# 224 unused bytes ahead of the activation tiles of a fused attention and feed-forward kernel

## The chip, the cores and the metric

The kernel runs on one core of one Trainium2 chip. The metric is the time of one execution on the device in microseconds. Lower is better. Engines are called PE (TensorE's matmuls), PEld (TensorE's weight loads), DVE (VectorE), ACT (ScalarE), POOL (GpSimd) and SP (SyncE, which issues the transfers).

## What is computed

Causal attention of 8 batches, 8 heads, 576 positions and 64 features, four heads with a local mask and four with a strided one, and behind it a feed-forward layer on 4608 tokens of 512 features with a hidden width of 2048:

```python
    scores = np.where(masks[None, :, :, :], scores, -1000000000.0)
    scores = scores - np.max(scores, axis=-1, keepdims=True)
    attn = np.exp(scores)
    attn = attn / (np.sum(attn, axis=-1, keepdims=True) + 1e-09)
    return np.matmul(attn, v).astype(np.float32)
...
    h = x @ w_in
    g = h * (1.0 / (1.0 + np.exp(-1.702 * h)))
    return (g @ w_out).astype(np.float32)
```

## The kernel before

The feed-forward layer is the bulk. Its tokens are cut into 9 groups of 512 (`NG`, `G`), its hidden width into 16 slices of 128 (`NF`), which makes 144 steps (`steps`, one for each group and slice). Every operand of a product is split into a high and a low part of type float32r, and a product is the sum of three matmuls (high with high, and each low part with the other's high part).

In step s, `ffn1` (line 474) makes the hidden slice `h`: 12 matmuls into one bank of the accumulator, 4 chunks of the features times 3 products. The stationary operand is a 128 by 128 piece of a weight tile `w`, the moving operand 512 tokens of `x` (tiles `xhl`, `xll`, `xhs`, `xls`: high or low part, local or strided heads). `act` (line 490) makes the activation in the tile `g2`, ACT first and DVE behind it; `split` (line 498) makes its high part `gh` on ACT and its low part `gl` on DVE. Two steps later (`LAG`), `ffn2` (line 506) multiplies it by the second weights: 12 matmuls, 4 pieces of 128 tokens times 3 products, into four banks `o`. Here the stationary operand is a piece of `gh` or `gl`, and the moving operand 512 columns of a weight tile `w`:

```python
            for m, (w, x) in enumerate(((wih, xh), (wih, xl), (wil, xh))):
                matmul(
                    hps[s], lhsT=w[f][:, c, :], rhs=x,
...
            for m, (g, w) in enumerate(((gh, woh), (gh, wol), (gl, woh))):
                matmul(
                    outs[i], lhsT=g[:, at], rhs=w[f],
```

So all 3456 large matmuls, 1728 named `h` and 1728 named `o` in the profile, have the same shape and type: 128 by 128 stationary, 128 by 512 moving. Each of them has a weight load of its own, which runs beside the matmul ahead of it.

The order of the work is written out by hand: every instruction is kept in program order on its engine (`InOrder`, line 106). A step of the main loop (line 652) issues `ffn1(s)`, then the work of ACT and DVE, then `ffn2(s - 2)`. The attention (`scores`, `maxima`, `softmax`, `transpose`, `values`) is cut into 42 pieces that are spread over the steps of the group before the one that needs them. The weights come as raw words, which ACT and DVE turn into the `w` tiles in the first 16 steps.

Tiles come from pools that lie one behind the other in each partition: const, wp, st, io, small, ffn. Within a pool the tiles lie in the order in which the code first asks for them. The build of this kernel places them as follows (first bytes in a partition, and what is left of them after division by 512):

| tiles | pool | bytes each | first bytes | modulo 512 |
|---|---|---|---|---|
| xhl, xll, xhs, xls | const | 8192, 8192, 12288, 12288 | 20192, 28384, 36576, 48864 | 224 |
| w, 32 buffers (also raw words, and the first q, k, v) | wp | 4096 | 61664 to 188640 | 224 |
| qk, 2 buffers | st | 4608 | 192736, 197344 | 224 |
| v, 2 buffers | io | 4096 | 210144, 214240 | 224 |
| nmax, ssum, rinv, 3 buffers each | small | 32 | 218336 to 218592 | 224 to 480 |
| g2 | ffn | 2048 | 218624 | 0 |
| gh, 2 buffers | ffn | 2048 | 220672, 222720 | 0 |
| gl, 2 buffers | ffn | 2048 | 224768, 226816 | 0 |

The nine small tiles take 288 bytes, which moves the byte from 224 to 0. All pieces that are read as an operand of a large matmul (512 bytes of `w`, `gh` or `gl` as the stationary one, 2048 bytes of `x` or `w` as the moving one) begin at a multiple of 512 bytes from the start of their tile.

Of the kernel before, what the change touches and what calls it, by code (L numbers as in the profile page):

```python
# [9 lines left out]
F32 = mybir.dt.float32  # L10
# [8 lines left out]
P = 128  # L19
# [44 lines left out]
def _pairs():  # L64

    def strided(b):
        return [("s", b, c) for c in range(len(NR))]

    def local(j):
        return [("l", LG * j + i, 0) for i in range(LG)]

    windows = []
    for j in range(NG - 1):
        a, b = strided(j + 1) if j + 1 < B else [], local(j + 1)
        windows.append([u for i in range(len(NR)) for u in a[i : i + 1] + b[i : i + 1]])
    return strided(0) + local(0) + [u for w in windows for u in w], windows
# [3 lines left out]
def attn_ffn(ctx, tc, lqk, sqk, lv, sv, w_in, w_out, masks, out):  # L82
# [7 lines left out]
    ffn = ctx.enter_context(tc.tile_pool(name="ffn", bufs=2))  # L90
# [8 lines left out]

    def st4(shape, dtype, name):  # L100
        return st.tile(shape, dtype, tag="st4", name=name, bufs=2)

    pairs, windows = _pairs()
    n0 = N0
# [27 lines left out]
    def load_qk(p):  # L132
        if p < len(pairs) and p not in qks:
            kind, a, c = pairs[p]
            src, n = (lqk[a], QKW[0]) if kind == "l" else (sqk[a * len(NR) + c], QKW[1])
            if p < N0 and kind == "s":
                qks[p] = w_tile([P, n], F32, f"qk_{p}")
            else:
                qks[p] = st4([P, QKW[0]], F32, f"qk_{p}")
            for i in (slice(0, n // 2), slice(n // 2, n)) if p == 0 else (slice(0, n),):  # L140
                sync.dma_start(out=qks[p][:, i], in_=src[:, i])
# [652 lines left out]
```

## Time and profile before

| | us |
|---|---|
| median of 3 runs | 907.83 (907.79 to 908.03) |
| span of the profiled execution | 905.2 |
| PE busy in it | 894.6 (99%) |
| DVE busy | 462.5 (51%) |
| ACT busy | 374.5 (41%) |

The span runs from the first to the last instruction of the program in one profiled execution; the median is 2.6 us above it, for what lies around it. Matmuls are pipelined and their shown ends reach beyond the start of the next one, so the time that a matmul takes in a dense row of them is read from one start to the next and not from its duration. The page gives every instruction the line of the helper that keeps the order (L116), so groups are told apart by the names of their tiles.

### The profile page before, as it was taken

What the parts mean: (1) busy time and instruction counts of PE and PEld (TensorE: products, weight loads), DVE (VectorE), ACT (ScalarE), POOL (GpSimd) and SP (SyncE); (2) the same over time, 40 slices, a digit from 0 to 9 for tenths busy, and PEclk for the clock granted to TensorE, in tenths of its full rate; (3) what the DMA queues carried; (4) which work ended last, traced back from release to release, by engine and by line L of the source; (5) the groups of instructions that cost most, each with busy time, mean ns of one, the idle gap of its engine ahead of it and who ended that gap; (6) DMA issues with size and microseconds to landing.
All of it is one profiled execution on the core that took longest, in us unless ns stands there. A gap on an engine that the chain in (4) does not pass through costs nothing.

```text
span 905.2 us, 14650 instructions
## 1 busy us (share of the span) xinstructions
PE 894.6 (99%) x5834; PEld 716.6 (79%) x5834; DVE 462.5 (51%) x886; ACT 374.5 (41%) x1129; POOL 55.4 (6%) x60
## 2 busy tenths in 40 slices
PE   8999999999999999999999999999999999999998
PEld 5777678888888888888888888888888888888886
DVE  4789966555454545554555555554555343323222
ACT  7798864343434333433434343434343332222221
POOL 4001001000000000010101001000001000000000
PEclk9999999999999999999999999999999999999999
DMA  9956223112121121211211211112120010001001
GB/s 277 347 214 231 76 74 104 39 39 76 51 68 38 35 76 46 57 54 44 79 39 38 78 60 58 38 42 82 33 78 23 18 47 1 1 1 47 0 1 47
DMA packets 21812, 62.42 MB, mean 69 GB/s; under 512 B 2608, under 2 KB 2992, under 8 KB 21744
## 3 DMA queue, kind: packets, MB, share of 16 engines
q1 hardware_dynamic: 21744, 61.49, 20.3%
q8 instruction: 46, 0.75, 0.3%
q14 instruction: 22, 0.18, 0.1%
HBM read 52.04 MB, written 9.44 MB: 68 GB/s over the span
## 4 chain that ended last, share of the span: by engine, by line
PE 90%; DVE 5%; ACT 3%; DMA 1%; issue 1%; DVEq 0%; ACTq 0%
PE o L116 42%; PE h L116 40%; PE a L116 4%; PE s L116 3%; DVE raw L116 1%; PE t L116 1%; ACT raw L116 1%; ACT pr L116 1%; DVE w L116 1%; DVE gl L116 1%; DMA raw<-w_out 1%; DVE pt_l L116 1%; DVE pr L116 0%; DVE pt_s L116 0%; ACT w L116 0%
## 5 line engine op out<-in xcount | busy, mean ns | idle before, releaser
L116 PE MATMUL o<-w,gh 128*128 128x512 f32 x1152 | 364.7, 398 | 0.0
L116 PEld LDWEIGHTS o<-w,gh 128*128 128x128 f32 x1152 | 213.8, 188 | 51.3
L116 DVE SCALAR_TENSOR_TENSOR g<-g,h 128x512 f32<-128x512 f32 x144 | 98.9, 687 | 268.5 <-ACT g L116 268.5
L116 PE MATMUL o<-w,gl 128*128 128x512 f32 x576 | 228.0, 396 | 0.0
L116 ACT ACTIVATE g<-h 128x512 f32<-128x512 f32 x144 | 85.9, 597 | 292.7 <-PE h L116 289.0
L116 PE MATMUL h<-xhl,w 128*128 128x512 f32 x576 | 202.9, 393 | 1.7 <-DVE w L116 0.9
L116 PE MATMUL h<-xhs,w 128*128 128x512 f32 x576 | 201.9, 391 | 0.4 <-ACT xhs L116 0.4
L116 DVE TENSOR_TENSOR gl<-g,gh 128x512 fp32r<-128x512 f32 x144 | 99.6, 692 | 129.1 <-ACT gh L116 126.7
L116 ACT CAST gh<-g 128x512 fp32r<-128x512 f32 x144 | 89.1, 619 | 184.7 <-PE o L116 176.5
L116 PEld LDWEIGHTS h<-xhl,w 128*128 128x128 f32 x576 | 107.8, 188 | 28.0 <-DVE w L116 2.4
L116 PEld LDWEIGHTS o<-w,gl 128*128 128x128 f32 x576 | 108.1, 188 | 25.9
L116 PEld LDWEIGHTS h<-xhs,w 128*128 128x128 f32 x576 | 108.2, 188 | 23.5 <-ACT xhs L116 0.8
L116 PE MATMUL h<-xll,w 128*128 128x512 f32 x288 | 112.4, 390 | 0.0
L116 PE MATMUL h<-xls,w 128*128 128x512 f32 x288 | 112.2, 389 | 0.1
L116 ACT ACTIVATE pr<-pr,nmax 128x96 f32<-128x96 f32 (+1 forms) x296 | 101.1, 346 | 0.0
L116 POOL TENSOR_TENSOR pr<-pr,rinv 128x432 f32<-128x432 f32 (+1 forms) x42 | 49.6, 1181 | 699.3 <-DVE rinv L116 699.3
L116 PEld LDWEIGHTS h<-xll,w 128*128 128x128 f32 x288 | 54.1, 188 | 11.8
L116 PEld LDWEIGHTS h<-xls,w 128*128 128x128 f32 x288 | 54.0, 188 | 11.7 <-DVE xls L116 0.4
L116 DVE STREAM_TRANSPOSE pt_l<-pr 32x256 f32<-32x256 f32 x128 | 55.5, 434 | 1.8
L116 ACT ACTIVATION_READ_ACCUMULATOR pr<-pr,nmax 128x1 f32 x296 | 56.3, 190 | 0.0
L116 DVE STREAM_TRANSPOSE pt_s<-pr 32x256 f32<-32x256 f32 x126 | 54.8, 435 | 1.8
L116 ACT ACTIVATE raw<-raw 128x512 f32<-128x512 f32 (+1 forms) x62 | 36.8, 666 | 2.4 <-DMA raw<-w_out 2.4
(64 smaller groups left out, 419.0 us busy)
## 6 DMA issues: line engine op xcount, KB each, us to landing
qk<-sqk SPq DMA_DIRECT2D x23, 452.0 KB, 4.0
qk<-lqk SPq DMA_DIRECT2D x18, 576.0 KB, 4.8
out<-out SPq DMA_DIRECT2D x36, 256.0 KB, 2.3
raw<-w_in SPq DMA_DIRECT2D x16, 512.0 KB, 8.4
raw<-w_out SPq DMA_DIRECT2D x16, 512.0 KB, 6.6
v<-lv SPq DMA_DIRECT2D x18, 384.0 KB, 3.7
v<-sv SPq DMA_DIRECT2D x24, 256.0 KB, 2.7
qk<-sqk SPq DMA_DIRECT2D x2, 226.0 KB, 2.7
```

The source lines that it names most:

```text
L116: ins = call(*args, **kw)
```

## The change

A tile of 56 float32 values (224 bytes in each partition) is asked for as the first one of the pool `ffn`. Nothing writes or reads it. The tiles `g2`, `gh` and `gl` are asked for behind it in the same pool, with tags of their own. No instruction is added, removed or moved.

```diff
     def st4(shape, dtype, name):
         return st.tile(shape, dtype, tag="st4", name=name, bufs=2)
+
+    ffn.tile([P, 224 // 4], F32, tag="fill", name="fill", bufs=1)
 
     pairs, windows = _pairs()
```

With the fill in front, `g2` would begin at byte 218848, `gh` at 220896 and 222944, `gl` at 224992 and 227040; all of these are 224 modulo 512.

## Rows read from the trace of the kernel before

**Rows 1.** The page: busy time of the engines, and the granted clock by slices.

```profile
PE 894.6 (99%) x5834; PEld 716.6 (79%) x5834; DVE 462.5 (51%) x886; ACT 374.5 (41%) x1129; POOL 55.4 (6%) x60
...
PEclk9999999999999999999999999999999999999999
```

**Rows 2.** Busy time by stretches: us, then each engine's (instructions), granted clock, DMA share, GB/s.

```profile
100.00:145.00 45.00, 43.23 (x276) 32.92 (x276) 35.00 (x64) 29.63 (x82) 3.26 (x3) 1.00 0.25 82
145.00:200.00 55.00, 55.00 (x377) 44.43 (x376) 28.84 (x61) 22.02 (x80) 3.85 (x3) 1.00 0.17 54
...
800.00:890.00 90.00, 90.00 (x392) 73.35 (x391) 23.70 (x35) 20.57 (x35) 0.00 (x0) 1.00 0.03 12
```

**Rows 3.** Matmuls of h and o by tile: ns shortest/median/longest, first and last start.

```profile
L116 PE MATMUL h<-xhs,w x120: 388/389/397, 723.1 to 887.0; 128*128 128x512 f32 x120
...
L116 PE MATMUL o<-w,gl x576: 389/396/397, 38.7 to 900.9; 128*128 128x512 f32 x192
```

**Rows 4.** Groups by line and form, PEld: busy us, mean ns of one | idle before.

```profile
L116 PEld LDWEIGHTS o<-w,gh 128*128 128x128 f32 x1152 | 213.8, 188 | 51.3
```

**Rows 5.** Timeline of PE in one step without attention: start us, us shown, what, count.

```profile
721.69 0.39 PE L116 MATMUL h<-xhl,w 128*128 128x512 f32 x1
...
722.15 0.62 PE L116 MATMUL h<-xhl,w 128*128 128x512 f32 x2
...
724.19 0.40 PE L116 MATMUL h<-xhs,w 128*128 128x512 f32 x1
724.42 0.62 PE L116 MATMUL o<-w,gh 128*128 128x512 f32 x2
724.88 0.40 PE L116 MATMUL o<-w,gl 128*128 128x512 f32 x1
...
726.98 0.40 PE L116 MATMUL o<-w,gl 128*128 128x512 f32 x1
727.22 0.39 PE L116 MATMUL h<-xhl,w 128*128 128x512 f32 x1
```

**Rows 6.** Timeline of the tail: two PE rows, and DVE's next work [idle before it].

```profile
897.41 0.40 PE L116 MATMUL o<-w,gl 128*128 128x512 f32 x1
...
898.81 0.40 PE L116 MATMUL o<-w,gl 128*128 128x512 f32 x1
...
899.25 0.69 DVE L116 TENSOR_SCALAR out<-o 128x512 f32<-128x512 f32 x1 [2.39 <-PE o L116]
```

**Rows 7.** Timeline of PE around one piece of attention.

```profile
218.57 0.73 PE L116 MATMUL o<-w,gh 128*128 128x512 f32 x2
219.14 0.40 PE L116 MATMUL o<-w,gl 128*128 128x512 f32 x1
...
221.48 0.39 PE L116 MATMUL h<-xhl,w 128*128 128x512 f32 x1
...
223.09 0.39 PE L116 MATMUL h<-xls,w 128*128 128x512 f32 x1
```

**Rows 8.** Scores from the two qk buffers: two pieces of attention, timeline of PE.

```profile
284.28 0.69 PE L116 MATMUL s<-qk 64*64 64x54 f32 x32
...
302.77 0.69 PE L116 MATMUL s<-qk 64*64 64x54 f32 x32
```

**Rows 9.** Groups by form, DVE and ACT: busy us, mean ns | idle before, what ended it.

```profile
L116 DVE TENSOR_TENSOR gl<-g,gh 128x512 fp32r<-128x512 f32 x144 | 99.6, 692 | 129.1 <-ACT gh L116 126.7
...
L116 DVE TENSOR_TENSOR xll<-a,xhl 128x512 fp32r<-128x512 f32 x16 | 11.1, 691 | 6.1 <-ACT xhl L116 6.1
...
L116 ACT CAST gh<-g 128x512 fp32r<-128x512 f32 x144 | 89.1, 619 | 184.7 <-PE o L116 176.5 <-DVE pt_s L116 7.5 <-DVE g L116 0.8
...
L116 ACT CAST w<-words 128x512 fp32r<-128x512 f32 x1 | 0.6, 620 | 1.4 <-DVE words L116 1.4
```

**Rows 10.** Waits of the whole span: who waited <- for whom: us, times, longest.

```profile
ACT g L116 <- PE h L116: 289.0, 126, 2.4
...
PE h L116 <- DVE w L116: 0.9, 3, 0.3
```

## The prediction

> **What bounds the kernel now.** I read the page first: PE is busy for 894.6 of the 905.2 us, and the granted clock is at its upper level, 2.4 GHz, in all slices [rows 1]. The table by stretches then says where PE has gaps: it is 43.23 of 45 us busy up to 145 us, and without a gap from there to 890 us [rows 2]. Of the waits, PE's own for other engines are around a microsecond each, while ACT waits 289 us for `h` [rows 10]. So from 145 us on the end is set by nothing but the time from one matmul to the next, and the 24 large matmuls of a step are nearly all of that.
>
> The question is then whether they all take the same. They have one shape and one type. The weight loads of `gh` take 188 ns [rows 4], and the five other groups of large weight loads have the same mean. In a step without attention, the third `h` matmul starts at 722.15 and the twelfth at 724.19: nine intervals in 2.04 us, 226.7 ns each. The third `o` matmul starts at 724.88 and the twelfth at 726.98: nine in 2.10 us, 233.3 ns each [rows 5]. The view by tile says the same for all of them: a matmul of `xhs` has a median of 389 ns, one of `gl` of 396 ns [rows 3]. So an `o` matmul costs 6.6 to 7 ns more than an `h` matmul, 1728 times.
>
> **Why that may hang on the byte.** What differs between `h` and `o`? I went through the candidates.
>
> - *The bank of the accumulator.* `h` stays in one bank for 12 matmuls, `o` changes it after every third. A cost of the change would fall on one interval of three. But the two intervals inside a bank, 724.42 to 724.88, already take 0.46 us, 230 ns each, against 226.7 [rows 5].
> - *Other engines on the same tiles.* DVE and ACT write `g2`, `gh` and `gl` while PE loads from them. At the end of the kernel they don't: DVE sits idle for 2.39 us up to 899.25, its work on `gl` long done, yet six `o` intervals from 897.41 to 898.81 take 1.40 us, 233.3 ns each [rows 6].
> - *Where in the partition the tile lies.* `gh` and `gl` are at the top, behind byte 220,000. The two `qk` buffers take turns, at 192,736 and 197,344, and the same 32 score matmuls take 0.69 us from either [rows 8]. That speaks against a slow region, weakly, since none of these is the region in question.
> - *The byte within 512.* For `h`, the stationary and the moving operand both begin at 224. For `o`, the moving one at 224 and the stationary one at 0. Nothing in the rows speaks against this one.
>
> One more thing speaks for operands that meet in the memory. After a change of partners the interval doesn't jump to its final value but settles: in one step with attention, the `h` matmuls start at 221.48 and only the eighth at 223.09, 230 ns each, before the pace is 226.7 again [rows 7]. A fixed cost of an instruction would not settle; two reads in step with each other would.
>
> **The change part by part.** *The fill itself* adds no instruction, no wait and no transfer; it takes 224 bytes at the end of the partition. Cost nothing, and there is no cover to lose.
>
> *DVE and ACT on the moved tiles.* DVE's `gl`, all operands at 0, takes 692 ns; its `xll`, written at 224, takes 691. ACT's `gh`, from 0 to 0, takes 619 ns; its one copy from `words` to `w`, from 224 to 224, takes 620 [rows 9]. So between a gain and a loss of 1 ns, 144 times, on engines that wait for PE: nothing.
>
> *The 1728 `o` matmuls.* Lower bound of the gain: none. Upper bound: all intervals of a step fall to 226.7 ns. A step is now 721.69 to 727.22, 5.53 us, of which 2.80 us begin with an `o` start [rows 5]. 24 times 226.7 ns is 5.44 us, 0.09 us less: 0.08 in `o`, 0.01 in the settling of `h`. From 145 us on there are 128 of the 144 steps: 128 times 0.09 is 11.5 us. Off this go the steps with attention, some 30 after 145 us. There, pairs must settle again, and the first two `o` intervals take 0.57 us [rows 7], for reasons that the byte doesn't touch. With 0.02 us each I take off 0.6 to 0.7. It leaves 10.8.
>
> In the first 16 steps the same 0.09 us would be 1.4 us, but PE waits there for converted weights [rows 2, 10]: 1.8 us of gaps between 100 and 145 us, which a faster PE only reaches earlier. Between 0 and 1.4 us, I take 0.2, since DVE is 35 of 45 us busy there and sets much of the pace. Sum 11.0 us: a span of 894.2 and, with the same 2.6 us around it, a median of 896.8.
>
> *What is late next.* Nothing near: a step would be 5.44 us, DVE has 23.70 us of work in the last 90 us and 28.84 in the densest 55, and ACT less [rows 2]. `gh` and `gl` are made two steps ahead.
>
> **Where the notes speak against it.** The `h` and `o` rows differ by 7 ns in matmuls that differ in nothing but their operands' places [rows 3, 5]. The Trainium skill's page "SBUF — State Buffer", section "Who interferes with whom", gives TensorE two independent read ports, one for the moving operand and one for weight loads, and says "PE and ACT never wait on anyone". The page "TensorE: Matmul & The Clock Gate", section "Step-by-step: what each phase is for", adds that loading the next weights takes no read bandwidth from the running matmul. By this the byte at which `gh` begins would be of no account, and the time would stay; the rival below has that as its mechanism. The trace agrees in that 188 ns of load are hidden; it doesn't say why `o` is slower.
>
> **The rivals.**
>
> 1. *No change, 907.8.* The `o` matmuls are slower for something that isn't the byte modulo 512, such as the top region itself or the moving `w` tile, or the fill, which no instruction uses, gets no room and nothing moves. For it: the first two `o` intervals behind `h` are 230 and not 233 ns [rows 5], although the stationary operand lies at 0 there too; and the interval from the last `o` to the first `h`, 726.98 to 727.22, is 0.24 us, although its stationary operand, a `w` tile, lies at 224 as the moving one does. Against it: the settling [rows 7] explains both. 0.19.
> 2. *Half way, about 902.* The pairs lock at another pace. The 230 ns of the first two `o` intervals [rows 5] is a pace that `o` does run at: 1728 times 3.3 ns is 5.7 us, 902.1. 0.10.
> 3. *Slower, about 910.6.* Moving `w` against a stationary operand at the same byte is tried in the trace only at the hand-over from `o` to `h`, and it is slow there (0.24 us). If the two reads collide there and stay locked, each `o` goes to the longest that a matmul at full pace shows, 397 ns [rows 3]. The mean of `o` without the starts behind attention is about 395.4, so 1.6 ns, 1728 times, 2.8 us. It decides from 1.05 ns per `o` matmul on, the 0.2% (1.8 us) that a measurement of this kernel can tell from no change. 0.09.
>
> **How the numbers follow.** Forecast 0.62, half way 0.10, no change 0.19, slower 0.09. The first two are faster by over 0.2%: 0.72, then 0.19 and 0.09. The forecast's own range is 895.3 (every settling gone, the first steps gain in full) to 898.5. The range for 8 in 10 has to reach over no change, so 895.0 to 908.3.
>
> **What would show it.** In the profile after: the median of `o<-w,gl` by tile at 389 and not 396; in a step without attention, `o` start to `h` start 2.72 us, not 2.80; no settling at the hand-overs, so the first `h` interval 227 ns too; `h` medians as before. The chain's share of `o` falls to that of `h`. If `o` stays at 396, the byte isn't the cause. If `o` falls but the span does not, the gain went into a wait of PE, and I have its slack wrong. The weakest step is that equality modulo 512 is enough: modulo 2048 `x` begins at 1760 and `w` at 224, so that `o` will not be the mirror of `h` in every bit.

## The result, and the profile after

The changed kernel took 898.02 us (median of 4 runs, 896.87 to 898.73) against 907.81 us, a ratio of 0.989 with a 95% interval of 0.9876 to 0.9904. The profiled execution has a span of 896.9 us against 905.2. The instructions are the same 14650, in the same order, and only `g2`, `gh` and `gl` lie 224 bytes further on.

The view by tile of the kernel after, for the matmuls and weight loads with `gl` and for the `h` matmuls with `xhs` (ns shortest/median/longest, first and last start):

```profile
L118 PEld LDWEIGHTS o<-w,gl x576: 187/188/188, 40.5 to 892.5; 128*128 128x128 f32 x192
L118 PE MATMUL o<-w,gl x576: 387/389/398, 40.7 to 892.7; 128*128 128x512 f32 x192
...
L118 PE MATMUL h<-xhs,w x120: 388/389/390, 723.0 to 884.5; 128*128 128x512 f32 x120
```

The median of `gl` fell from 396 [rows 3] to 389 ns, that of `xhs`; the weight load stayed at 188 [rows 4]. One step without attention, PE's timeline:

```profile
721.42 0.39 PE L118 MATMUL o<-w,gl 128*128 128x512 f32 x1
721.65 0.39 PE L118 MATMUL h<-xhl,w 128*128 128x512 f32 x1
...
724.37 0.62 PE L118 MATMUL o<-w,gh 128*128 128x512 f32 x2
724.82 0.39 PE L118 MATMUL o<-w,gl 128*128 128x512 f32 x1
...
725.50 0.39 PE L118 MATMUL o<-w,gl 128*128 128x512 f32 x1
```

From the third `o` start to the sixth it is 0.68 us, 226.7 ns each, where [rows 5] had 233.3; the `h` half of the step takes 2.72 us and no longer settles at its beginning. From 145 us on PE has no gap, as before, and the other engines have the load that they had [rows 2, 10]:

```profile
ACT g L118 <- PE h L118: 287.0, 126, 2.3
...
145.00:200.00 55.00, 55.00 (x380) 44.93 (x379) 29.21 (x61) 22.06 (x77) 3.85 (x3) 1.00 0.19 65
```

**Where the profiled difference went.** From the first `gl` matmul to the last one it was 38.7 to 900.9 us [rows 3], 862.2 us; it is 40.7 to 892.7 now, 852.0. That is 10.2 us less. But the span fell only by 8.3, because the first `gl` matmul came 2.0 us later; what was late lies ahead of the first matmul on the moved tiles. The table by stretches shows where (granted clock is the number ahead of the last two). First the kernel before, then the one after:

```profile
20.00:25.00 5.00, 4.02 (x26) 2.98 (x25) 2.85 (x5) 2.69 (x13) 2.17 (x3) 0.66 1.02 348
31.00:35.00 4.00, 4.00 (x28) 3.32 (x25) 2.37 (x5) 2.92 (x6) 0.00 (x0) 1.00 1.03 403
```

```profile
20.00:25.00 5.00, 2.70 (x28) 1.97 (x28) 3.33 (x7) 3.06 (x17) 2.52 (x3) 1.00 1.03 345
31.00:35.00 4.00, 4.00 (x35) 3.35 (x31) 2.41 (x5) 2.30 (x4) 0.00 (x0) 0.57 1.04 406
```

In both executions PE runs for a short stretch at the lower level of 1.2 GHz (the rows mix it with 2.4 GHz). The slices of [rows 1], 22.6 us each and all at 9, are too long to show it. Before, this lay in 20 to 25 us, where PE had pauses between pieces of attention. After, it lay in 31 to 35 us: PE had paused for 1.12 us up to 30.07, then came attention and the first of 30 `h` matmuls that run without a pause up to the first `o`. The same five intervals of `h`, and the attention ahead of them, before and then after:

```profile
30.23 1.15 PE L116 MATMUL a<-pt_l,v 96*64 96x64 f32 x30 [0.27 <-DVE pt_l L116]
31.31 0.50 PE L116 MATMUL h<-xhs,w 128*128 128x512 f32 x1
...
32.57 0.39 PE L116 MATMUL h<-xhs,w 128*128 128x512 f32 x1
```

```profile
30.67 1.66 PE L118 MATMUL a<-pt_l,v 96*64 96x64 f32 x30 [0.27 <-DVE pt_l L118]
...
32.26 0.80 PE L118 MATMUL h<-xhs,w 128*128 128x512 f32 x1
...
34.54 0.39 PE L118 MATMUL h<-xhs,w 128*128 128x512 f32 x1
```

The `h` intervals take 2.28 us in place of 1.26, the attention 1.59 in place of 1.08. That is 1.5 of the 2.0 us, where the lower clock lies; the rest was lost before. Whether the fill does that was a question for the runs.

### The profile page after: what moved, and what is told of

Its sections match the earlier page's. It is cut to its first block, busy times and chain, and to the rows that moved or that the text cites. A ratio compares the mean times of both kernels' runs of the same rounds, so it can differ in the third digit from the quotient of the medians.

```text
span 896.9 us, 14650 instructions
## 1 busy us (share of the span) xinstructions
PE 884.5 (99%) x5834; PEld 716.4 (80%) x5834; DVE 463.1 (52%) x886; ACT 375.1 (42%) x1129; POOL 55.7 (6%) x60
## 4 chain that ended last, share of the span: by engine, by line
PE 89%; DVE 5%; ACT 4%; DMA 1%; issue 1%; SPq 0%; DVEq 0%; ACTq 0%
PE o L118 41%; PE h L118 41%; PE a L118 4%; PE s L118 3%; DVE raw L118 1%; ACT pr L118 1%; ACT raw L118 1%; DVE w L118 1%; DMA qk<-sqk 1%; DVE gl L118 1%; DVE pt_l L118 1%; DMA raw<-w_out 1%; DVE pr L118 0%; DVE pt_s L118 0%; PE t L118 0%
## 5 line engine op out<-in xcount | busy, mean ns | idle before, releaser
L118 PE MATMUL o<-w,gh 128*128 128x512 f32 x1152 | 359.1, 393 | 0.0
L118 PE MATMUL o<-w,gl 128*128 128x512 f32 x576 | 224.4, 390 | 0.0
L118 ACT ACTIVATE g<-h 128x512 f32<-128x512 f32 x144 | 86.0, 597 | 290.7 <-PE h L118 287.0
```

Of the source, the lines that this page charges most:

```text
L118: ins = call(*args, **kw)
```

## The experiments

I held two theories of the gain against each other. By the first, the *distance* of the two operands counts: the byte of the stationary operand minus that of the moving one, modulo something. By the second, the stationary operand's *own* byte counts, and 0 is a bad one. A third, that `o` is slow for its banks or for its place at the top of the partition, was all but out with the result, but one run bears on it too. The measure is the time from the first to the last `gl` matmul, which leaves the beginning out: 862.2 us before, 852.0 after.

**The same kernel again.**

> The changed kernel once more, unedited, for its spread and a second profile. Theory A (the first 40 us vary from run to run, whatever the fill): this profile has its stretch of half clock elsewhere, the first o matmul starts within 1 us of the 38.2 of before, and the time is 896.5 to 898.5. Theory B (the fill itself costs 1.5 to 2 us at the start): the first o matmul starts at 40.0 to 40.4 again, the time is 897.8 to 898.8 in all rounds.

899.02 us, 896.66 to 900.83, against 909.25 us for the kernel before beside it (907.04 to 911.35); the ratio is 0.9888, 0.9868 to 0.9908. Its rows:

```profile
L118 PE MATMUL o<-w,gl x576: 387/389/398, 41.0 to 893.0; 128*128 128x512 f32 x192
...
31.00:35.00 4.00, 3.94 (x36) 3.40 (x37) 2.49 (x5) 2.23 (x5) 0.00 (x0) 0.57 1.03 387
```

Again 852.0 us from first to last, and again a late start, so A was wrong about this profile: the first `o` start came at 40.6. The median of the times lies above its range, too. But B was wrong about the rounds, which spread over 4 us, as those of the kernel before do. The next three runs say more on this.

**Other sizes of the fill.** From here on each kernel was run once, with its profile. The edit is one number:

```diff
-    ffn.tile([P, 224 // 4], F32, tag="fill", name="fill", bufs=1)
+    ffn.tile([P, 32 // 4], F32, tag="fill", name="fill", bufs=1)
```

> A fill of 32 bytes in place of 224: g2, gh and gl begin at 32 modulo 512, 192 bytes (3 times 64) short of w and x. Same modulo 512 needed: the median of o<-w,gl is 396 ns as before the change, time about 908. Same modulo 64 is enough: 389 ns, 898. The byte of the stationary operand alone counts, and 0 is the bad one: 389 ns, 898.

> A fill of 192 bytes: gh and gl begin at 192 modulo 512, 32 bytes short of w and x. Same modulo 512 or modulo 64 needed: 395 to 396 ns for o<-w,gl, about 908. Same modulo 32 is enough, or only a start at 0 is bad: 389 ns, 898.

> A fill of 480 bytes: gh and gl begin at 480 modulo 512, 256 bytes past w and x. Same modulo 512 needed: 396 ns, about 908. Same modulo 64, 128 or 256 is enough, or only a start at 0 is bad: 389 ns, 898.

The `gl` matmuls with fills of 32, 192 and 480 bytes:

```profile
L118 PE MATMUL o<-w,gl x576: 390/395/398, 38.9 to 903.1; 128*128 128x512 f32 x192
...
L118 PE MATMUL o<-w,gl x576: 388/394/397, 39.4 to 900.8; 128*128 128x512 f32 x192
...
L118 PE MATMUL o<-w,gl x576: 387/389/398, 39.1 to 891.1; 128*128 128x512 f32 x192
```

With 32 it is 864.2 us from first to last, with 192 861.4: both about as slow as before (909.16 and 906.83 us in all). So 0 is not a bad byte of its own, and an equal remainder modulo 32 or 64 is not enough. With 480, 256 bytes away from equality, it is 852.0 (897.13 us in all): equality modulo 512, as the change was put, asks for more than is needed.

The fill of 480 also speaks against a fill as the cause of the late start: it starts `gl` at 39.1 us, and its stretch at the lower clock begins early, as that of the kernel before does:

```profile
20.00:25.00 5.00, 3.56 (x26) 2.65 (x26) 3.31 (x7) 3.30 (x18) 2.52 (x3) 0.76 1.02 340
31.00:35.00 4.00, 4.00 (x41) 3.35 (x37) 2.73 (x5) 2.52 (x5) 0.00 (x0) 1.00 1.06 411
```

Kernels with the gain start early or late, and so do kernels without it: the first `gl` matmul comes at 38.7 us before, at 43.0 with the fill of 96 below. In the five profiles whose stretch at 1.2 GHz lies behind about 31 us (both of the changed kernel, the fills of 64 and 96, and the kernel of 16 bytes below, which has no fill at all) it is 13.2 us from the first `h` start to the first `o` start; in the other eight it is 9.9 to 11.5. So neither the fill nor the distance decides it. Both profiles of the changed kernel are late, so whether it varies between executions of one kernel is not shown; what sets it, I did not test.

**Distance or own byte.**

> A fill of 96 bytes: gh and gl begin at 96 modulo 512, 128 bytes short of w and x. Fills of 224 and 480 gave 389 ns, of 0, 32 and 192 394 to 398. Same modulo 128 is enough: 389 ns for o<-w,gl, steady part as with 224, time 897 to 899. Same modulo 256 is needed: 394 to 398 ns, 906 to 909.

> x, w, gh and gl all begin at 0 modulo 512 (288 unused bytes ahead of them all, the small pool moved behind ffn). The distance of the two operands counts: 389 ns for h and for o, 897 to 899. The stationary operand's own byte counts, and 0 is bad: 395 ns or more for both, some 10 us above the kernel before, 917 to 920.

> w, gh and gl begin at 0 modulo 512, x stays at 224 (288 unused bytes between x and w, the small pool behind ffn). The distance of the two operands counts: the roles change, o has both at 0 and falls to 389 ns, h has 0 against 224 and rises to 395 or 396 ns; the time is that of the kernel before, 906 to 909. The stationary operand's own byte counts: both at 395 ns or more, 917 to 920. Something in g's place or in the banks of o makes o slow: h 389, o 396.

> A fill of 160 bytes: gh and gl begin 64 bytes short of w and x. Same modulo 128 (or 256) needed: 394 to 398 ns, 905 to 909. If the fill of 32 was slow for its size of distance (192 bytes) and not for the remainder, 64 bytes are nearer to none: between 389 and 394 ns.

The edits of the second and the third of these, against the kernel before (in both, the pool `small` is moved behind `ffn`):

```diff
+    const.tile([P, 288 // 4], F32, name="fillc")
     prs = [const.tile([P, HU, KB], F32, name=f"pr_{i}") for i in range(AHEAD)]
```

```diff
+    wp.tile([P, 288 // 4], F32, tag="fill", name="fill", bufs=1)
+
     pairs, windows = _pairs()
```

The matmuls of the fill of 96, of all at 0 (`gl`, then `xhs`), of `w` and `g` at 0 (`gl`, then `xhs`), and of the fill of 160:

```profile
L118 PE MATMUL o<-w,gl x576: 388/393/404, 43.0 to 907.3; 128*128 128x512 f32 x192
...
L116 PE MATMUL o<-w,gl x576: 387/389/398, 39.7 to 891.7; 128*128 128x512 f32 x192
...
L116 PE MATMUL h<-xhs,w x120: 388/389/389, 722.0 to 883.5; 128*128 128x512 f32 x120
...
L118 PE MATMUL o<-w,gl x576: 387/389/398, 40.1 to 904.8; 128*128 128x512 f32 x192
...
L118 PE MATMUL h<-xhs,w x116: 395/396/397, 720.9 to 880.0; 128*128 128x512 f32 x116
...
L118 PE MATMUL o<-w,gl x576: 388/388/398, 39.1 to 894.3; 128*128 128x512 f32 x192
```

All at 0 is fast throughout: 852.0 us from first to last, 897.67 us in all. With `w` and `g` at 0 against `x` at 224 the roles change, as the theory of the distance said: `gl` has a median of 389 ns and `xhs` of 396, and the time is back (864.7 us from first to last, 910.79 in all, a little above the 906 to 909 that I had expected). The own byte is out. So are the banks of `o` and the place of `g` in the partition: `g` lies at the very bytes of the kernel before and `o` goes through its banks as there, yet `o` is fast.

Two hand-overs in the timeline of this kernel, with `w` and `g` at 0:

```profile
719.31 0.39 PE L118 MATMUL o<-w,gl 128*128 128x512 f32 x1
719.54 0.40 PE L118 MATMUL h<-xhl,w 128*128 128x512 f32 x1
...
722.34 0.63 PE L118 MATMUL o<-w,gh 128*128 128x512 f32 x2
...
725.09 0.40 PE L118 MATMUL h<-xhl,w 128*128 128x512 f32 x1
```

Here the 12 matmuls of `h` take 2.80 us and the 12 of `o` 2.75, of which 2.72 would be the fast pace: `o` settles for a while after each `h`.

The fill of 96, 128 bytes short, is slow: 864.3 us from first to last. It also started late (43.0), which makes its 913.29 us, more than expected. The fill of 160, 64 bytes short, is nearly as good as equality: 855.2 us and 900.41 in all. By the distance modulo 128 it should have been as slow as the fill of 32, which is 64 past (864.2). So 64 bytes short and 64 bytes past are not alike: the sign counts too. The expectation had a place for it, 389 to 394 ns, but the median came out at 388, below that of equality. The intervals are longer all the same:

```profile
719.71 0.62 PE L118 MATMUL o<-w,gh 128*128 128x512 f32 x2
...
722.24 0.39 PE L118 MATMUL o<-w,gl 128*128 128x512 f32 x1
```

From the first `o` start to the twelfth it is 2.53 us, 230 ns each, against 226.7 after the change. So the shown durations don't rank the kernels; the starts do.

**Closer to equality, and the rest of the circle.** In the first of these (without the fill, and with the pool `small` behind `ffn`), `gh` and `gl` lie in one tile, with an unused piece ahead of them whose size makes the distance 16 bytes modulo 256 in both buffers:

```diff
-        gh, gl = gs[s] = [
-            ffn.tile([P, G], F32R, tag=f"g{x}", name=f"g{x}_{s}", bufs=LAG) for x in "hl"
-        ]
+        n = (4, 60)[s % 2]
+        gs2 = ffn.tile([P, n + 2 * G], F32R, tag=f"gs{s % 2}", name=f"gs_{s}", bufs=1)
+        gh, gl = gs[s] = [gs2[:, n + i * G : n + (i + 1) * G] for i in range(2)]
```

> gh and gl lie in one tile per parity of the step, each 16 bytes past the remainder modulo 256 of the moving w (no other distance so far was under 32). Equality to the byte is needed: over 390 ns for o, o intervals 229 to 234, 900 to 909. What counts is the remainder in units of 32 bytes or more: 389 ns, 226.7, 897 to 899. A distance that is not 0 can be better than 0: under 388 ns, under 896.

> A fill of 64 bytes, the stationary operand 96 bytes past the moving one modulo 256. Only 0 modulo 256 is good: 392 to 398 ns for o, 903 to 910. The pace is a matter of the distance to 192, which gave 229 ns: not worse than 233.

> A fill of 128 bytes, the stationary operand 160 bytes past the moving one modulo 256. Only 0 modulo 256 is good: 390 to 398 ns for o, 900 to 910. As the neighbour of 192 (229 ns) it may be between: 229 to 233 ns.

The `o` matmuls of the 16 bytes, and the `gl` matmuls of the fills of 64 and 128:

```profile
L116 PE MATMUL o<-w,gs x1728: 387/389/499, 40.4 to 893.9; 128*128 128x512 f32 x192
...
L118 PE MATMUL o<-w,gl x576: 390/397/400, 40.6 to 904.8; 128*128 128x512 f32 x192
...
L118 PE MATMUL o<-w,gl x576: 389/392/399, 39.8 to 906.0; 128*128 128x512 f32 x192
```

At 16 bytes the median is that of equality, and the whole took 900.01 us, 1 us above what was expected for it. From its first `o` matmul to its last it is 853.5 us; the changed kernel has 852.4 between the same two (40.23 to 892.67). So the pace is reached, with 1.1 us lost on the way to it. The fills of 64 and 128 are slow (864.2 and 866.2 us from first to last, 910.87 and 912.08 in all, both a little above the 910 expected); being the neighbour of 192 does not help 160. By the distance modulo 256, then, counted as the stationary operand past the moving one:

| distance | kernel | first to last `gl`, us |
|---|---|---|
| 0 | fill 224, fill 480, all at 0 | 852.0 |
| 32 | before | 862.2 |
| 64 | fill 32 | 864.2 |
| 96 | fill 64 | 864.2 |
| 128 | fill 96 | 864.3 |
| 160 | fill 128 | 866.2 |
| 192 | fill 160 | 855.2 |
| 224 | fill 192 | 861.4 |

The four profiles at 0 (the changed kernel has two) agree to 0.1 us. The measure takes in the `h` half of each step, and in some of the slow kernels that half settles too: in one step of the fill of 128, ten intervals of `h` take 2.30 us (719.99 to 722.29), in one of the fill of 160 they take 2.26 (717.00 to 719.26). No distance tried was better than 0, so no kernel of these beats the changed one.

## Why the prediction was right

- *The byte is the cause.* The forecast rested on the one difference of `h` and `o` that no row spoke against. The runs show it: with the roles exchanged, `h` takes the 396 ns and `o` the 389.
- *The pace after.* 226.7 ns and a median of 389 were forecast, and both came, with an equal first `h` interval. The term of 0.09 us for a step without attention stands: 721.65 to 724.37 is 2.72 us for `h`, and three `o` intervals at 0.68 us make 2.72 for the twelve.
- *The size.* 11.0 us were forecast, 896.8 us; 9.8 were measured in the first comparison and 10.2 in the second. The term that was too small is the settling behind a piece of attention, for which 0.02 us a piece were taken off. A step of the kernel after shows what it is:

```profile
670.54 0.69 PE L118 MATMUL s<-qk 64*64 64x54 f32 x32
671.16 0.74 PE L118 MATMUL o<-w,gh 128*128 128x512 f32 x2
671.74 0.40 PE L118 MATMUL o<-w,gl 128*128 128x512 f32 x1
...
673.14 0.39 PE L118 MATMUL o<-w,gl 128*128 128x512 f32 x1
```

  From 671.74 to 673.14 there are six intervals in 1.40 us, 233 ns each: the equal remainder sets the pace that is reached, not how soon. These six alone lose 0.04 us. Worked back from the whole: the `h` matmul that starts at 142.55 us before starts at 144.19 after, 104.3 and 104.0 us behind the first `o` start (38.2 and 40.2), so 0.3 of the 10.2 us fall before it. Of the 128 steps behind it 32 have attention ahead of their `o` matmuls; the other 96 make 8.6 us at 0.09. That leaves 1.3 us for the 32, 0.04 each, where the forecast had 0.07. That is 1.0 us in all, a little more than the whole difference between 11.0 and 10.2; the 0.1 us too few for the first steps goes the other way.
- *The first steps.* 0.2 us were put down for the first 16 steps, and with the 0.3 above that was about right. What moved there by more, 2.0 us in the profiled execution, was no part of the sum: the first 40 us vary by that much between the profiles of like kernels, and I had no term for that. The range did not need its reach up to no change: 898.02 lies within the forecast's own 895.3 to 898.5, if by 0.5 us only. (By the terms of the sum, 11.5 and 1.4, the lower end of that range is 894.9.)
- *DVE and ACT at nothing.* Right from 145 us on: PE has no gap there, and ACT's wait for `h` is 287.0 us after 289.0 [rows 10]. In the first 45 us PE's waits are 6.0 us after 4.5, most of the difference for DVE's `pt_l`, which is no tile that moved.
- *The rivals.* "No change" had two rows for it, the 230 ns of the first two `o` intervals behind `h` and the 0.24 us of the hand-over from `o` to `h` [rows 5]. In the kernel after, where no distance changes, they are 0.45 us for two and 0.23 us (724.37 to 724.82, 721.42 to 721.65), which agrees with settling; with `w` and `g` at 0 it is `o` that settles behind each `h`. The half-way pace of 230 ns exists, 64 bytes short, but not here. The slower rival did not come about, but its place is real: other distances do cost more than the 32 bytes that the kernel before had by chance.
- *The Trainium skill against it.* By the Trainium skill's page "SBUF — State Buffer", section "Who interferes with whom", TensorE's two read ports are independent and it waits for no one. The trace agrees in that the weight load takes 188 ns at either distance. But the interval is 6.6 ns longer at a distance of 32 bytes than at 0, so the places of the two operands do count. The measurement decides.
- *What stayed weak.* "Modulo 512" was called the weakest step. It holds, but 256 is enough, and 16 bytes past, the pace is still reached.

What is shown is that the distance of the two operands sets the pace, and that 256 bytes are as good as 0; whether the other distances repeat every 256 bytes as well was not tried. That the two reads meet in parts of the memory is an inference from the table. It is open, too, which two reads these would be: a matmul's own two operands, or its moving one and the weights that are loaded beside it for the next. In a row of like matmuls both pairs have the same distance, so no run here tells them apart.

## What to carry to other kernels

Where PE runs without a gap, compare the interval from start to start of matmuls that have the same shape but different operands; a few nanoseconds, 1728 times, are 10 us. For float32r matmuls like these (128 by 128 stationary, 128 by 512 moving; no others were tried), whose weight load runs beside the matmul ahead, let the stationary and the moving operand begin at the same byte modulo 256, and look at where the pools put them before the order of instructions is changed. A handful of small tiles between two pools is enough to spoil it.

## What was not expected of the hardware

- The pace settles over several matmuls after a change of partners and behind attention, and the distance decides which pace it settles to: 226.7 ns at 0, 16 and 256 bytes.
- The circle isn't symmetric: 64 bytes short (855.2 us) is nearly as good as 0 (852.0), 64 bytes past (864.2) is not.
- A short stretch at 1.2 GHz, 31 to 35 us into the profiled execution (granted 0.57 on the mean of these 4 us) in place of 20 to 25 us (0.66), comes with a first `gl` matmul some 2 us later. Where it falls differs between the profiles of like kernels, so a profile's span alone can misjudge a change of 1%.
